# A frequency mixer and a two-layer network on one core: tokens stored n1 outside and n2 inside, and the order table rewritten

## The chip, the cores and the metric

The kernel runs on one core of a Trainium2 chip. A core has a TensorE for matrix products, a VectorE (DVE in the profile), a ScalarE (ACT) and a GpSimd (POOL) for elementwise work, a SyncE (SP) that issues transfers, and 16 DMA engines that carry them. SBUF holds the tiles on chip, in 128 partitions; PSUM takes TensorE's results, in eight banks of 512 fp32 columns per partition; HBM is the memory outside. The metric is the device time of one execution in microseconds (us). The three runs before the change took 845.41, 846.81 and 847.99 us, a median of 846.81.

## The reference

The input x is 8 sequences of 3008 tokens with 256 channels. A first part mixes in the frequency domain, a second is a network applied to each token. All in float32, with `w_in` of 256 x 2048 and `w_out` of 2048 x 256:

```python
X = np.fft.rfft(x, axis=1)
Yr = Xr @ w_r - Xi @ w_i + b_r
Yi = Xr @ w_i + Xi @ w_r + b_i
Yr = np.sign(Yr) * np.maximum(np.abs(Yr) - 0.01, 0.0)   # and Yi likewise
y = np.fft.irfft(Yr + 1j * Yi, n=3008, axis=1)
h = y.reshape(24064, 256) @ w_in
g = s * np.maximum(h, 0.0) ** 2 + b
out = g @ w_out                                         # 24064 x 256
```

## The kernel before

**The transform.** A sequence's 3008 tokens are laid out as n = 32 n1 + n2, with n1 from 0 to 93 and n2 from 0 to 31, and the transform over n is split into one over n1 and one over n2, each a matrix product with a constant table. For each batch (one sequence) there are four steps:

- `s1_units`: x (loaded by POOL's queue) times `A_t` over n1 gives u, which is evicted, written to the HBM buffer `ud` by SP and read back in another order as four loads `us`.
- `s23_units`: `fwd_unit` transforms `us` over n2 into xf, `sum_unit` and `mix_unit` apply the channel weights in three products, `shrink` does the soft threshold with three VectorE operations in the tile `ring`. Four small SBUF to SBUF transfers (`ring<-ring`, issued by SP; copies on VectorE for the last pairs of a batch) then exchange halves of the partitions, and `inv_unit` (matmuls `ring,T_t`) transforms back over n2 into v. v goes to HBM as `vd`, and two half loads `vs` bring it back in another order.
- `s4_units`: `vs` times `C_t` transforms back over n1. For up to five n2 at a time one PSUM bank takes 5 x 94 columns, and an eviction (`leave_bank`, a cast on ScalarE or VectorE) puts them into the tile `yt`, which holds y transposed: channels in the partitions, tokens along the row. For batches 2 to 7 a POOL copy puts the tokens with n1 from 80 to 93 into `tail`, shared by two batches.

Batch 0 goes through `first_batch`, which keeps it on chip; its first transposed result `ut` is evicted with a permuted access pattern already.

**The network.** The tokens are cut into 48 tiles of up to 512 (`_tile_order`): "wide" ones of batches 0 and 1 (16 n2 by 32 or 30 n1), "main" ones (32 n2 by 16 n1) and "tail" ones. `first_mm` makes h in PSUM (`psh<-yt,w_in`, 16 times two matmuls for each tile), each pair of banks is passed through a relu into `rt` and a square into `gt`, on ScalarE or VectorE, and the next tile's slots run the second product. In `second_mms` that is sixteen matmuls for each sub-tile of 128 tokens, into half a `psa` bank. In `seven_mms`, used for 21 tiles, seven products on sums of blocks stand in for eight; the sums are made by `s_op` on VectorE, and the fourth of them by an accumulating transfer on POOL's queue (`gt<-gt`, L1282). VectorE leaves the result in one of three tiles `ost` with two sub-tiles each, and `store` sends it to HBM by SP. A sub-tile's 128 tokens were eight n2 by sixteen n1 in a main tile, so a store's rows lay 32 rows apart in the output; two sub-tiles took two transfers. In tail tiles a sub-tile was cut at whole n2, into three pieces or so.

**The order.** The program of TensorE is one fixed list of 7662 matmuls, in which `plan` and `schedule` place the transform's units among the network's. Everything that the other engines and queues do from the second batch on is a "piece" made by `later`. Each engine, and each queue that issues transfers, works strictly in the order in which its pieces are issued, and waits at the head for what the piece needs. That order is written out by hand in `TURNS`, two characters in base 36 for every piece:

```python
at = [divmod(int(TURNS[k : k + 2], 36), 4) for k in range(0, len(TURNS), 2)]
... for k in sorted(range(len(at)), key=lambda k: k + at[k][0])
```

The quotient says by how many pieces the piece is put off, the remainder which engine does it (0 ScalarE, 1 VectorE, 2 SP, 3 POOL). `pump`, called ahead of every matmul, issues the pieces in that order as far as they have been made. Nothing else places the work: a load that the table issues late is late.

The functions that the diff touches, with what calls them:

Of the kernel before, what the change touches and what calls it, by code (L numbers as in the profile page):

```python
# [10 lines left out]
F16 = mybir.dt.float16  # L11
# [4 lines left out]
P = 128  # L16
N1 = 94
# [9 lines left out]
    "25253y20241x21251w26241s24242e1p2h3m363m2q1d20181c1k1x1o1h20213g1g1x251w30232j231s1g1s1t3o1s"  # L27
    "2x341t222a1k1k1t1k1t1w1x2w1w2d1x21252p4i5u2m2y143c1c1h1h1p1t1x2a66425m0o1h101c2x1c2c191i2q15"
    "191h1h1q5e2m320k111c1l111p1x215i4u222y0o1k2o0s3p0s191x25255662262m0g340h1d0d0g2q101t10181x3a"
    "2i2l0l1t25314e5y324y091m080w3c590h10390w1g4x0x191p1t2q1q3652044i0h0g1d0k1p0p151t1x5i522m5i0g"  # L30
    "3y0k0o1o11221a0k0s291c2s111h1t2h2i4m3m4u0h1a0k0w3c0z0x1p19252529462i52220g0o0w0p321820382h2y"
    "3a11191d1h2h2x193x082y0w143t151h212l31312d2d0x1m0s1431194a142g1g1s1u1s2c2d2q2u1d1k1w2i362u15"
    "1t1d3y181x1l2h251k2d1l1u2m20221k291x2l1k25241s2d213a1w20212a2e1x211k34212b1o301s2l2v1p1t2l1g"
    "1k2o1h2d1l2u1w291l1x2035251u2h5h1s2t1p1p1o1t1s2l1s1s3u1s2c2h2h1h2q3e1i1q102d45101k2w181d1h2d"
    "2n1c1l1c2o1m2x371l1p1x1p1g381w251l1s251x20291w3k1v2t2t1t1x1x313a3i4i3q101g191t0w1c1w1l2x131l"
    "1o201l2t1l2y3i1y2u2l2t11151c2g191h3x414e4q4a4y21270k200s1x2b0x0x1l113d0k1w191d0w28141g2w1d2h"
    "1b1l2x414h4y5e524e0w1s0x151c1i111w1d1c241d1l111m1u121y11211d1c311g1o2g1s1x1h1w2x1x2d35393q3a"
    "463m18421542102t111a1i0s10102p1525142h15144m1c1g2w1w2h1x1o1s2t323a1h1p1t294a2u3m2u0r1c1s0w2m"
    "0t2y1019281h1l1k211l2028353i3m1p1t1x293x2d3t353p2d3l2d0o0u0x120k25150w1g1h4i1o2s1c1x321s1w29"
    "2e2m1d1g1h2s1k2i321t22191l1k2s1x1w1w292u2a2e1l4e1g1t252d1o201t2021252e1s201t262e252t1l1o251t"  # L40
    "2x331s1s3o1s2p371l1p1x1c1g291o2l1o1q1s291t24242h21461x2p1s1w1w212d1p1s1w2k1w1z461s251p1p2l2a"
    "1q2i2u1l2p1o2k181l31371h1l1c2s5m1p292r1h1l35182h182g1l2p1g1p1g341l1p25292y2m3e221418241b1c2t"
    "1d3o1t211h1o251s2821253p3t56463y3m131d1c1x1d1l111u22121a182x1d142s1c1g341g1x1l2t3539524a4i36"
    "0s2o0x1215143g112q2a101x0x0w240z151h2s1c1l1p292d2l464e2m2u182h0x2m1d1c1s1h2q2610251p1c1x1k2c"
    "2g1s251p252h2h2p2u46323e1d42182s152218181c2d1l2a32111c1d5q1o3d1l1p25292h3l3d2t2t2x1p290k0o14"
    "1d4u0n1452142s1c1o1p2s1p2i1y181e1c1d521h241p2q3m1h1g1l1k1q1g1w1k1t2k1x2i1y1g2i2a1c1x1d2l411t"
    "211o3i1s2k1t1s211p1y2a1g1u2l2p1l3g1k1k2t2z1k1o351o2l331h1l2t181c2p1d2t1o1i1o2l1s1w1w30241u25"
    "2p1s1w2s1t1t1s281x2g1s234q1x241x251x3a3m261q3d3t1g1s1d1h1x271d1d1c2k1e2l2z1d1d2d1p1c341s2d25"
    "1o2d1p1x2d1s291v4t5121252l2t3u2y4e32101c1d1d0s181c1d2l4z1l141g111h1h3e2m1u2m2d3h0s1d0w281d2p"
    "3p3x4a5a4q4a151j0c2s0k1t230p0t1x142p0g10250x102c191c3c1o25131p292l2p3m323q2m182s0x191d3e101l"  # L50
    "1c1k2k1l1p1t3a2m2q261c3l1d1h2h1k1p311o2h1l1s2k1p1t2d353q4a4a3q0w4e104a1c1w1p1y220x0w0x240s2l"
    "141c151d2q1h1h1t1s2p2c1s2l252a2u1h2p353h3q4m3e420r1c1s101a112y1d1c2g191k1838151c4d2h322i151d"
    "1l1x2p4d2d411p392929082a151m041w1l0s1w1o461t2t1o1p3u1k1w292q2a1d1h1g281x2a3e192e181l1s2x241s"
    "241p2a1q2a2l2q1h1w1x2h1s2s1t1w21202q1w251t222e2h3l1o1s241t252b1t1w3k1w2h2r1p1t291g1k2t1o2h1s"
    "1u1s2c1p20252l204q21311o1s2t21251k1l1o1w1p5z3y1s1s1x211l262q1i3a1l1p182k1g1p213f181l1c2t261l"
    "1v1l1x211k1o2c212h291k281l252d20283v1t5p1x1x21293m322q2618291d1l10181k202h171t1s2829291l2u3m"
    "4a2q4u1y4a4u1a2e0m2u1t210p0x0k1o0p2x454d564m5a4a1h1r041w0k151z050d210s1p001s1l0t10251d1g1o20"
    "2d171t252d2h363q422e102c1t2114221429181s2c2d2d1h322m2e1a182t1t1k2s1t1s2x1w2h1l1s2p1p2d2p3d52"
    "4i4a3u114e104i101k1x262a0s0s142l0t0x101k15181e1d1g2t1p2p1k1s242d322m1h292d2l2y2q3u3a0r18390w"
    "2a182e1c1c2o1h1l1k1w1p28382l2q3e1l1p1t212x4d3h3t213h1l310k1m10220c1o151d1p1g4a1g2o1k1t3e1o1w"  # L60
    "1x2q2y1d1p1p1x1k1m3i1k3y1k1t1w2p1t1t1w1p2e1u2y1h2a1g2s1p1x1k1w20212g21321w251t2a1y2p2x1o1w3h"
    "1l1t271o1s3c1w2d2n1p1t2l1g1k381k291o1q242c1t1w1x351w4i1x1w2o1t1t1s201o2c1l1z4e1t1x212l1x2y32"
    "1u2y1429181h181p1g1s4e1w1x251s2d1w201t20251w243z2l451l361q2i1u363i111921293u4a3e3q0c0o0t0w1o"
    "181l0r1x1k1x1h2y1i353t1p1t183k1l212t3p524i3q3y0x1b0s141c1x270x11210w3l0w1s2111141s1d1x241w29"
    "1f1t292x313a565a3e1c1p1d1p1842181c1g1k211p29192u2e1y1i101p1p142w1k1l251k2l1l1w2k1t292h2t424i"
    "362q153u141e1g34252i2a1110141c112p1c2s1h1g4i1l1o2c1s2l1p1t242l2u361l1t393h423e4e3y0n101s0x12"
# [1455 lines left out]
```

## Time and profile before

| | |
|---|---|
| runs | 845.41, 846.81, 847.99 us |
| profiled execution | 845.85 us, its span 844.1 us |
| TensorE busy | 821.6 us, 97% |
| VectorE busy | 729.1 us, 86% |
| ScalarE busy | 705.8 us, 84% |
| POOL busy | 84.5 us, 10% |
| issues on SP's hardware queue | 100578 packets, 80.55 MB, 33.5% of the 16 DMA engines' span |
| stores of the output | 228 issues by SP |

The span is the time from the first to the last instruction of one execution; the execution's own time has 1.75 us around it. Each engine's busy time leaves out waits and the issuing of transfers. A group in the profile is named by engine, operation and tiles: `psh<-yt,w_in` is a matmul from yt and w_in into a PSUM tile psh. Behind a vertical bar stand the group's busy time in us and the mean of one in ns, and behind a second bar how long the engine had been idle ahead of them, and what ended that. In a list of waits the numbers are the total in us, how many times, and the longest. In the table of stretches each row has the stretch, its length, the busy time of TensorE, of its weight loads, of VectorE, ScalarE and POOL, each with its number of instructions, and then the granted TensorE clock as a share of full speed, the DMA engines' share and GB/s. For one tile the three durations in ns are the shortest, the median and the longest. The chain follows the work that ended last back from the end; its columns are start, duration and what it was.

### The profile page before, as it was taken

The numbers are of one execution on the slowest core, as the hardware profiler recorded it, in microseconds if no ns is written. First come the engines' busy times: TensorE is split into PE (matmuls) and PEld (weight loads), VectorE is DVE, ScalarE is ACT, GpSimd is POOL, SyncE is SP. The second block draws the span as 40 slices with busy tenths as digits, with TensorE's granted clock in tenths as the row PEclk, the third lists the DMA queues.
The fourth block names the chain that finished last, engine by engine and source line by source line (L and its number), as shares of the span: only waits on it lengthen the run. The fifth ranks groups of instructions, "written<-read, shape, count | busy, mean of one in ns | idle before, by whom it ended". The sixth has DMA issues, their size and how long they took to land.

```text
span 844.1 us, 19222 instructions
## 1 busy us (share of the span) xinstructions
PE 821.6 (97%) x7662; PEld 601.3 (71%) x7662; DVE 729.1 (86%) x1178; ACT 705.8 (84%) x888; POOL 84.5 (10%) x112
## 2 busy tenths in 40 slices
PE   8999999999999999999999999999999999999997
PEld 7857767777676767777677766767667777767765
DVE  5987889989898889999889889889879988889794
ACT  4988978998888888887899887988899988879773
POOL 4530000110012000110001100100002000011000
PEclk8999999999999999999999999999999999999999
DMA  8954537655458347574466543654556432623321
GB/s 198 177 153 97 125 109 191 133 132 124 116 142 179 100 119 216 115 148 115 114 162 159 126 123 108 168 143 110 133 161 158 92 88 66 162 56 65 77 66 54
DMA packets 114748, 107.14 MB, mean 127 GB/s; under 512 B 10854, under 2 KB 98922, under 8 KB 113314
## 3 DMA queue, kind: packets, MB, share of 16 engines
q1 hardware_dynamic: 100578, 80.55, 33.5%
q0 software_dynamic: 14080, 25.37, 18.4%
q8 instruction: 60, 0.98, 0.5%
q14 instruction: 30, 0.25, 0.1%
HBM read 53.52 MB, written 46.66 MB: 119 GB/s over the span
## 4 chain that ended last, share of the span: by engine, by line
PE 77%; DMA 11%; DVE 7%; ACT 3%; issue 1%; SPq 1%; POOL 0%; DVEq 0%; ACTq 0%; POOLq 0%
PE psh L235 31%; PE psa L235 28%; PE psf L235 16%; DMA ring<-ring 3%; DMA vs<-vd 3%; DMA gt<-gt 2%; DMA vd<-v 2%; PE psm L235 1%; DVE gt L1138 1%; ACT rt L1125 1%; ACT gt L1136 1%; DVE ring L891 1%; DMA x<-in_x_dram 1%; DVE rt L1127 1%; DMA us<-ud 1%
## 5 line engine op out<-in xcount | busy, mean ns | idle before, releaser
L235 PEld LDWEIGHTS <-gt 128*128 128x128 f16 (+1 forms) x3696 | 305.0, 101 | 170.1 <-DMA gt<-gt 2.9
L235 PE MATMUL psh<-yt,w_in 128*128 128x512 f16 (+1 forms) x1344 | 397.5, 378 | 1.2 <-DVE yt L298 0.8
L1125 ACT ACTIVATE rt<-psh 128x1024 f32<-128x1024 f32 (+2 forms) x322 | 323.8, 1007 | 72.7 <-PE psh L235 67.6
L235 PE MATMUL psa<-w_out_t,gt 128*128 128x256 f16 (+3 forms) x2448 | 310.0, 253 | 2.4 <-DMA gt<-gt 2.4
L1136 ACT ACTIVATE gt<-rt 128x1024 f16<-128x1024 f32 (+2 forms) x249 | 256.0, 1042 | 6.6 <-DVE rt L1127 4.5
L1138 DVE TENSOR_TENSOR gt<-rt 128x1024 f16<-128x1024 f32 (+2 forms) x135 | 161.2, 1202 | 5.7 <-ACT rt L1125 5.1
L235 PEld LDWEIGHTS <-w_in 128*128 128x128 f16 x1536 | 136.3, 98 | 28.0 <-issue 5.2
L1127 DVE TENSOR_SCALAR rt<-psh 128x1024 f32<-128x1024 f32 (+1 forms) x62 | 74.1, 1197 | 21.3 <-PE psh L235 14.9
L1282 POOL DMA_DIRECT2D gt<-gt x42 | 38.3, 938 | 514.3 <-DVE yt L298 93.1
L235 PE MATMUL psa<-T_s,gt 128*128 128x128 f16 (+1 forms) x944 | 79.4, 219 | 0.0
L891 DVE TENSOR_TENSOR ring<-psf,s 128x512 f16<-128x512 f32 x84 | 57.6, 686 | 21.4 <-PE psf L235 15.8
L235 PE MATMUL psh<-tail,w_in 128*128 128x512 f16 (+1 forms) x192 | 52.1, 353 | 0.0
L235 PEld LDWEIGHTS <-xf 128*128 128x128 f16 x504 | 46.9, 98 | 5.3 <-DVE xf L851 0.8
L235 PE MATMUL psf<-W_g,xf 128*128 128x256 f16 x336 | 50.4, 273 | 0.0
L298 DVE CAST u<-psf 96x512 f16<-96x512 f32 x53 | 36.0, 680 | 8.7 <-PE psf L235 8.5
L1225 DVE SCALAR_TENSOR_TENSOR ost<-psa,s_bc,bias_bc 128x512 f32<-128x512 f32 (+2 forms) x51 | 36.9, 723 | 6.5 <-PE psa L235 4.8
L298 ACT CAST xf<-psf 128x512 f16<-128x512 f32 x59 | 34.1, 583 | 8.9 <-PE psf L235 8.8
L235 PE MATMUL psf<-x,A_t 94*96 94x512 f16 x102 | 38.9, 382 | 0.9 <-DVE ring L891 0.5
L235 PE MATMUL psf<-C_t,vs 96*128 96x94 f16 (+1 forms) x484 | 37.7, 205 | 2.1 <-DMA vs<-vd 2.1
L298 ACT CAST yt<-psf 128x470 f16<-128x470 f32 (+2 forms) x70 | 35.7, 519 | 4.2 <-PE psf L235 2.9
L1325 DVE SCALAR_TENSOR_TENSOR ost<-psa,s_bc,zz 128x256 f32<-128x256 f32 (+1 forms) x80 | 36.2, 478 | 3.2 <-PE psa L235 2.0
L298 ACT CAST v<-psf 128x512 f16<-128x512 f32 x43 | 25.0, 583 | 14.2 <-PE psf L235 14.2
(121 smaller groups left out, 887.0 us busy)
## 6 DMA issues: line engine op xcount, KB each, us to landing
out_dram<-ost SPq DMA_DIRECT2D x152, 128.0 KB
ud<-u SPq DMA_DIRECT2D x56, 192.0 KB
us<-ud SPq DMA_DIRECT2D x28, 384.0 KB
vd<-v SPq DMA_DIRECT2D x42, 256.0 KB
vs<-vd SPq DMA_DIRECT2D x14, 768.0 KB
x<-in_x_dram POOLq DMA_DIRECT2D x28, 376.0 KB, 7.4
gt<-gt POOLq DMA_DIRECT2D x38, 256.0 KB, 4.7
ring<-ring SPq DMA_DIRECT2D x120, 64.0 KB
```

Source lines behind the costliest of these rows:

```text
L235: return nc.tensor.matmul(out, lhs, rhs, **how)
L298: (nc.scalar.copy if e == "act" else nc.vector.tensor_copy)(out=dst, in_=src)
L891: lambda e: nc.vector.tensor_tensor(out=ring[0][:, i % 4], in0=ps, in1=hold[i // 2][:, i % 2].unsqueeze(1).to_broadcast([P, 2, D]), op=ALU ...
L1125: nc.scalar.activation(out=rt, in_=ps[:, :, 0:w], func=AF.Relu)
L1127: nc.vector.tensor_scalar(out=rt, in0=ps[:, :, 0:w], scalar1=0.0, scalar2=None, op0=ALU.max)
L1136: nc.scalar.activation(out=gt, in_=rr, func=AF.Square)
L1138: nc.vector.tensor_tensor(out=gt, in0=rr, in1=rr, op=ALU.mult)
L1225: nc.vector.scalar_tensor_tensor(out=osts[number % 3][0:size, 0:k], in0=ps[0:size, 0:k], scalar=s_bc[0:size], in1=bias_bc[0:size].unsqueez ...
L1282: nc.gpsimd.dma_start(out=a12, in_=a11, accum_op=ALU.add)
L1325: nc.vector.scalar_tensor_tensor(out=out, in0=of, scalar=s_bc[0:size], in1=other, op0=ALU.mult, op1=ALU.add)
```

## The change

`yt` and `tail` hold the tokens with n1 outside and n2 inside. The evictions into `yt` read the PSUM bank in permuted order and write for each n1 the four or five n2 that the bank holds. A main tile's 16 n1 by 32 n2 tokens are then 512 neighbouring elements of the row, in the order of the output's rows. `store` is called once for two sub-tiles, and sends 256 consecutive rows by one transfer where it can; wide tiles keep one for each sub-tile, or two where a sub-tile ends inside an n1. All of `TURNS` is replaced: 2440 entries in place of 2525; the 85 that are gone are stores. The matmuls and their order stay.

```diff
@@ first_batch, last_dft
-        yt = yts[0] = ypool.tile([P, DC, N2, 96], F16, name="yt", tag="yt")
+        yt = yts[0] = ypool.tile([P, DC, 96, N2], F16, name="yt", tag="yt")
...
-                yt[:, ec, n : n + 4, :], ps,
-                ps[:, 0:384].rearrange("p (j n) -> p j n", n=96), 384,
+                yt[:, ec, :, n : n + 4], ps,
+                ps[:, 0:384].rearrange("p (j n) -> p n j", n=96), 384,
@@ s4_units
-                yt[:, ec, n2 : n2 + w, 0:N1], ps,
-                ps[:, 0 : w * N1].rearrange("p (j n) -> p j n", n=N1), w * N1,
+                yt[:, ec, 0:N1, n2 : n2 + w], ps,
+                ps[:, 0 : w * N1].rearrange("p (j n) -> p n j", n=N1), w * N1,
...
-                        out=tails[pr][:, :, half], in_=yt[:, :, :, 80:94]
+                        out=tails[pr][:, :, half], in_=yt[:, :, 80:94, :]
@@ rhs_of
-            return yts[b][:, dc, HW * h : HW * h + HW, lo : lo + w]
+            return yts[b][:, dc, lo : lo + w, HW * h : HW * h + HW]
         if kind == "main":
-            return yts[b][:, dc, :, 16 * j : 16 * j + 16]
-        return tails[b][:, dc].rearrange("p h n m -> p (h n m)")[:, j : j + w]
+            return yts[b][:, dc, 16 * j : 16 * j + 16, :]
+        return tails[b][:, dc].rearrange("p h m n -> p (h m n)")[:, j : j + w]
@@ store
-    def store(tl, sub, number, i, op):
-        src = osts[number % 3][:, i, :]
+    def store(tl, sub, k, number, op):
+        src = osts[number % 3]
...
         if kind == "wide":
             h, lo = j
-            n2 = HW * h + 4 * sub
-            rows = out[b * N : (b + 1) * N, :].rearrange("(n1 n2) d -> n2 n1 d", n2=N2)
-            send(rows[n2 : n2 + 4, lo : lo + w], src[0 : 4 * w])
+            rows = out[b * N : (b + 1) * N, :].rearrange("(n1 n2) d -> n1 n2 d", n2=N2)
+            rows = rows[:, HW * h : HW * h + HW]
+            for i in range(k):
+                t = (sub + i) * size
+                end = t + size
+                while t < end:
+                    n1, n2 = divmod(t, HW)
+                    whole = n2 == 0 and end - t >= HW
+                    cnt = (end - t) // HW * HW if whole else min(HW - n2, end - t)
...
         if kind == "main":
-            rows = out[b * N + 512 * j : b * N + 512 * (j + 1), :]
-            send(rows.rearrange("(n1 n2) d -> n2 n1 d", n2=N2)[8 * sub : 8 * sub + 8], src)
-            return
+            runs = [(b * N + 512 * j + P * sub, P * k)]
+        else:
...
+        if len(runs) == 1 and runs[0][1] == P * k:
+            rows = out[runs[0][0] : runs[0][0] + P * k]
+            send(rows.rearrange("(i p) d -> p i d", p=P), src[:, 0:k])
+            return
...
@@ second_mms
-                for i in range(k):
-                    store(tl, sub - k + 1 + i, number, i, op)
+                store(tl, sub - k + 1, k, number, op)
@@ seven_mms, leave
-                    for j in range(2):
-                        store(tl, 2 * i + j, hold["o", 3 * i], j, op)
+                    store(tl, 2 * i, 2, hold["o", 3 * i], op)
@@ the table, its first entries
-    "25253y20241x21251w26241s24242e1p2h3m363m2q1d20181c1k1x1o1h20213g1g1x251w30232j231s1g1s1t3o1s"
+    "28292i242d21282g2l2q1w1x2h252i1o2h3e3m423m1k281k1o1o281t1h251k301h1s29202d371j3b251o21243h1s"
```

## The prediction, written before the result was known

> **What bounds the kernel now.** I read the first part of the page, then the busy time by stretches, then TensorE's waits, the chain in order of time, and the groups that the change rewrites.
>
> ```profile
> PE 821.6 (97%) x7662; PEld 601.3 (71%) x7662; DVE 729.1 (86%) x1178; ACT 705.8 (84%) x888; POOL 84.5 (10%) x112
> ```
>
> ```profile
> 58.00:200.00 142.00, 139.73 (x1268) 103.32 (x1267) 126.05 (x222) 123.41 (x160) 10.79 (x15) 1.00 0.57 134
> 200.00:400.00 200.00, 194.61 (x1789) 141.72 (x1788) 178.50 (x287) 167.78 (x209) 15.79 (x20) 1.00 0.57 141
> 400.00:600.00 200.00, 197.03 (x1811) 142.42 (x1809) 177.24 (x284) 174.06 (x217) 15.49 (x20) 1.00 0.55 134
> 600.00:800.00 200.00, 199.12 (x1906) 144.17 (x1905) 173.10 (x269) 172.97 (x205) 14.42 (x16) 1.00 0.42 106
> ```
>
> TensorE is the bound: busy 139.7 of 142, 194.6 of 200, 197.0 of 200, 199.1 of 200 us, at a granted clock of 1.00. No matmul is added or dropped, so a gain can only come from TensorE's pauses. From the matmuls' starts (each form has one usual distance to the next; the excess is a pause) the pauses sum to 26.0 us, 15 of them after us 58. TensorE's waits name the enders:
>
> ```profile
> PE psf L235 <- DMA ring<-ring: 2.7, 4, 1.2
> PE psa L235 <- DMA gt<-gt: 2.4, 3, 0.9
> PE psf L235 <- DMA vs<-vd: 2.1, 3, 1.3
> PE psf L235 <- DVE xf L298: 1.5, 1, 1.5
> ...
> PE psf L235 <- DMA us<-ud: 0.7, 1, 0.7
> ```
>
> Four kinds of transfer that land late. Counted by matmul starts, pauses behind a late transfer are 9.7 us after us 58: ring copies 3.4, gt sums 2.85, vs loads 2.55, us loads 0.9. The chain shows how long such landings last:
>
> ```profile
> 223.81 5.01 DMA vd<-v
> ...
> 228.90 5.86 DMA vs<-vd
> ...
> 265.34 7.29 DMA ring<-ring
> ...
> 332.31 7.65 DMA gt<-gt
> ```
>
> Each queue works in the order that the table gives: if the table puts a transfer 7 us ahead of its matmul and it needs 8.5, TensorE pauses 1.5.
>
> **The change part by part.** The sum is made against the profiled execution's own 845.85 us (span 844.1, 1.75 around it), 0.96 below the median of 846.81.
>
> *Layout of yt.* The matmuls read 512 neighbouring elements in place of 32 runs of 16.
>
> ```profile
> L235 PE MATMUL psh<-yt,w_in 128*128 128x512 f16 x1216 | 361.0, 379 | 1.2 <-DVE yt L298 0.8 <-DVE rt L1127 0.2
> L235 PE MATMUL psh<-tail,w_in 128*128 128x512 f16 x96 | 28.6, 379 | 0.0
> L249 DVE CAST ut<-psf 128x384 f16<-128x384 f32 x8 | 4.5, 558 | 8.1 <-PE psf L235 8.0
> L298 DVE CAST yt<-psf 128x384 f16<-128x384 f32 x4 | 2.2, 545 | 0.0
> ```
>
> The tail is read in one run today and costs 379 ns as well: worth 0. The evictions into yt now read PSUM by jumps and write runs of 5 (of 4 in the first batch). The ut eviction does that with runs of 4: 558 ns against 545 on VectorE; on ScalarE 479 against 485 to 489. So about +13 ns for each of some 39 on VectorE, 0.5 us in all, and -6 to -10 ns on ScalarE: hidden, as between an eviction's end and the matmul that needs it the trace leaves a median 0.8 us (under 0.4 us in 9 of 102). If every one took 0.25 us more, those gaps would let through 0.2 us. I take 0; ends -0.1 and +0.5, the upper for runs of 5, which no row shows. [...] POOL's six tail copies (median 1.17 us) are issued 26 us or more before use: 0.
>
> *Stores.* From the code: 228 issues become 143. Main tiles: 59 of 256 rows and 2 of 128 for 120 of 128; tails 18 for 60; wide tiles 64 for 48, since a sub-tile of 120 tokens no longer ends on a whole n1 and is sent as 112 + 8.
>
> ```profile
> L1162 SPq DMA_DIRECT2D out_dram<-ost x228: 248/609/1142, 65.3 to 840.0; - x114
> L966 SPq DMA_DIRECT2D vd<-v x42: 355/424/936, 89.6 to 717.7; - x42
> ```
>
> SP issues stores for 135 of its 307 us. The nearest row for a 256 KB store is vd's write (256 KB from 128 partitions, 0.42 us); a store keeps 0.61 at the worst. 65 x 0.42 + 48 x 0.61 + 30 x 0.35 = 67 us, or 80 with 0.61 throughout: 55 to 68 us less on SP, which was not the bound (307 of 844). On the path lies only what queues behind stores. By the trace's landing records a main store took a median 3.1 us and its semaphore climbed in 9 steps, a wide one 5.2 us in 5 steps, vd's write 3.3 us in 16 steps for twice the bytes; I read the steps as 8, 4 and 16 DMA engines at work. Two stores of 3.1, the second issued 0.6 later, become one of about 3.3. Half a us less in front of a ring copy takes a quarter to a third off the late sum of the ring copies; I take -0.7 us (ends 0 and -2.5).
>
> *The table.* Two characters per piece of work in base 36; the number over 4 is by how many pieces it is put off, the remainder its engine. Old and new first entries, "25" and "28", are 77 and 80: 19 pieces late on VectorE, 20 late on ScalarE. I decoded both, matched the pieces (2525 less 85 stores is 2440), and took as slack the time from the matmul in front of which a transfer is issued to the matmul that needs it, in the profile's matmul starts:
> - vs loads: shortest slack 6.8 us, now 9.4; under 9 us: 5 of 14, now 0. With the needs measured (queueing plus landing, 6.5 to 12.0) the late sum falls from 8.9 to 2.0 if needs and slacks are combined at random, so three quarters of 2.55: -2.0 us. One at us 234.8 (1.47 us) keeps its 10.3 us, as its v write lands late.
> - us loads: the late one at us 553.5 has 14.1 us in place of 6.5: -0.8.
> - gt sums: the late ones at us 340 and 374 gain 1.5 and 1.6 us of slack, that at 790.5 none: -2.1 where they stand, -1.3 by the same random pairing (2.04 to 1.13). I take -1.3.
> - ring copies: the shortest goes from 3.4 to 5.2, but more groups are near the edge: the last copy of a group has under 7 us in 24 of 40, before in 17. At random the late sum falls 16%, -0.5; with each copy's own lateness kept it grows from 2.5 to 8.0, +5.5. The copies' new neighbours on SP are fewer, which speaks for the first; I take 0, ends -3.4 and +5.5.
> - engines: 12 relus and 8 evictions go to VectorE, 5 squares back: 12 x 1.22 + 8 x 0.68 - 5 x 1.23 - 0.7 = +13 us on VectorE (86 to 88% busy), some -13 on ScalarE. Six pieces (squares, ring moves on VectorE, sums of the seven products) now have less slack than they took, together 3 us; each lay in another order, so I take +1.0 (ends 0 and +3). What is late next is psa's leaving: shortest slack 3.3, now 2.2 us, against 0.7 to 2.9 taken.
> - the end: the last out's store still stands ahead of two ready ones; the third starts 0.2 to 0.4 sooner: -0.3 (ends +0.3 and -1).
>
> A 3.15 us VectorE square at us 450.3 (usual 1.23) beside POOL's tail copy cost the wait on xf, 1.5 us; it may go or recur: 0, ends -1.5 and +1.5.
>
> Sum: 0 - 0.7 - 2.0 - 0.8 - 1.3 + 0 + 1.0 - 0.3 = -4.1; 841.75 in the profile's own terms, with 0.96 back 842.7 at the median: 842.5.
>
> **The rivals.**
> - *The ring copies turn late* (slower). Place: TensorE's ring,T_t matmuls of batches 1 to 7. For it: 24 of 40 groups under 7 us while half of them need 5 or more; VectorE, which runs the shrink ahead of them, is fuller by 13 us. Against: fewer stores, less time in front of them. Price: +5.5 with each copy's lateness, +10.4 with half a us more; with the other terms' -4.1 + 0.7 that is +2.1 to +7, so 849 to 854. It decides where the copies land, against their plan, as late as today.
> - *The pauses only change places.* The late transfers go and others come, within 2.5 us: 844.5 to 849. For it: both tables fill VectorE over its time in some stretches of 20 us, and the pauses before were placed by chance too. Against: the slacks of vs and us grew at every short place.
> - *Spread stores carry more.* If the stores on few engines are what stretches ring copies to 7.29 us (median 2.6), all four kinds shorten: -9.7 of late transfers, -1 at the end, 836 to 838. [...]
> - *Slow evictions.* If the runs of 5 cost 0.4 us more, 84 of them put 34 us on two engines that are idle 14 to 16%; the gaps let through 0.8 us directly, a tenth of the load 3 more: 847.
>
> **How the numbers follow.** What a measurement of this kernel tells from no change is 0.3%, 2.5 us: 844.3 and 849.4 are the bounds. Forecast (839 to 844.2): 0.58. Spread stores: 0.06. Changed places: 0.15, taken as the same. Ring copies late: 0.17, slower, 0.02 of it inside the bound. Slow evictions or some other stretch: 0.04, slower in most. So faster 0.63, same 0.17, slower 0.20. The range from 838 to 851 leaves out the better half of the spread case and the worse half of the ring case, less than 2 in 10; the forecast's own is 839 to 844.
>
> **What would show it.** In the profile after: the waits of TensorE on vs and us gone but for one near us 235, gt at most one; psh<-yt still 379 ns; yt evictions 545 to 560 ns (ScalarE) and 640 to 660 (VectorE); out_dram<-ost x143, near 0.42 us for the large ones; ring copies' waits at 2 to 4 us. Wrong it would be with ring waits above 6 us, waits of psa matmuls on VectorE's ost, or evictions over 0.75 us.

## The result and the profile after

The changed kernel took 836.2 us (835.52, 836.88, 838.0, 834.68) against 846.11 us for the kernel before (845.41, 846.81, 847.99, 844.2): a ratio of 0.9884 with a 95% interval from 0.9852 to 0.9916. Two later comparisons of the same two kernels gave 0.9864 (0.9833 to 0.9895) and 0.9871 (0.9842 to 0.99). So it is faster by 1.2 to 1.4%, some 10 to 11 us, where 4 us were forecast, and its time lies below the predicted range. One slow execution, 1218.26 us of the kernel e10 below, is left out of all figures. The profiled execution is the one of 835.52 us, with a span of 833.7. The profile's first part, then TensorE's busy time by stretches (the columns as before: stretch, length, busy time and instructions of TensorE, its weight loads, VectorE, ScalarE and POOL, then clock, DMA share and GB/s):

```profile
PE 818.9 (98%) x7662; PEld 598.5 (72%) x7662; DVE 736.8 (88%) x1192; ACT 702.2 (84%) x874; POOL 83.4 (10%) x112
```

```profile
58.00:200.00 142.00, 141.44 (x1286) 105.38 (x1285) 127.39 (x226) 126.71 (x164) 10.04 (x14) 1.00 0.55 129
200.00:400.00 200.00, 197.98 (x1805) 143.30 (x1803) 182.34 (x292) 171.36 (x209) 16.00 (x20) 1.00 0.56 138
400.00:600.00 200.00, 199.36 (x1830) 144.41 (x1829) 181.41 (x290) 172.15 (x215) 14.88 (x20) 1.00 0.55 140
600.00:800.00 200.00, 199.37 (x1921) 143.99 (x1919) 179.86 (x277) 168.59 (x194) 14.77 (x17) 1.00 0.39 102
```

TensorE pauses for 0.56, 2.02, 0.64 and 0.63 us in the four stretches; before it was 2.27, 5.39, 2.97 and 0.88. VectorE is a little fuller, 88% in place of 86. TensorE's waits (total in us, times, longest):

```profile
PE psf L234 <- DMA ring<-ring: 1.3, 2, 0.8
...
PE psf L234 <- ACT yt L297: 0.6, 2, 0.3
PE psa L234 <- DMA gt<-gt: 0.6, 2, 0.4
```

The rows for vs, us and xf, 2.1, 0.7 and 1.5 us before, are gone from the list, and gt went from 2.4 to 0.6, ring from 2.7 to 1.3.

**Three parts of the span.** All the kernels below run the same 7662 matmuls in the same order, so a span can be cut by them: *start* up to matmul 600 (there the first batch's evictions into yt differ, in runs of four that take as long as before, and with the new order also the order of each engine's last dozen or so operations), *middle* from there to the start of the last matmul, *end* from there on.

| profile of | start | middle | end | span |
|---|---|---|---|---|
| before | 62.1 | 775.7 | 6.2 | 844.1 |
| after | 60.5 | 768.5 | 4.8 | 833.7 |
| after, second profile | 61.2 | 767.3 | 4.8 | 833.2 |
| after, third profile | 64.6 | 767.5 | 4.8 | 836.9 |

The start varies by itself, 60.3 to 64.6 us over all profiles here, so the 1.6 us at the start, of 10.3 between the first two profiles, tell nothing of the change. The middle gave 7.2 to 8.4 us, the end 1.5. The pauses in the middle, counted by matmul starts as in the prediction, can be sorted in two ways. By what ended them, those behind late transfers were 3.4 us for ring copies, 2.85 for gt sums, 2.55 for vs and 0.9 for us loads; in the three profiles after they are 1.0 to 1.9, 0.5 to 1.2, 0 and 0. By the matmul that paused, whatever ended its wait, they went so: matmuls on vs from 2.6 to 0.9, second products (psa) from 2.9 to between 1.6 and 2.2, matmuls on ring from 4.6 to between 2.5 and 3.0, matmuls on us from 1.5 to 0.6, and one wait of 1.7 us on a VectorE result at us 454 is gone. What is left at the matmuls on vs is no vs load: those waits end with ScalarE evictions into yt. Pauses at vs, gt, ring or us below are sorted in this second way.

**What was left alone, and what grew.** Groups with their count, busy time, mean in ns and the idle time ahead of them, of the changed kernel:

```profile
L234 PE MATMUL psh<-yt,w_in 128*128 128x512 f16 x1216 | 360.8, 379 | 1.5 <-ACT u L297 0.8 <-DVE rt L1124 0.3 <-ACT rt L1122 0.2
L297 ACT CAST yt<-psf 128x470 f16<-128x470 f32 x52 | 34.0, 683 | 2.9 <-PE psf L234 2.7
L297 DVE CAST yt<-psf 128x470 f16<-128x470 f32 x32 | 22.4, 704 | 3.4 <-PE psf L234 3.4
L297 DVE CAST yt<-psf 128x384 f16<-128x384 f32 x5 | 2.7, 546 | 0.0
L297 ACT CAST yt<-psf 128x384 f16<-128x384 f32 x4 | 2.0, 488 | 1.5 <-PE psf L234 1.5
```

and of the kernel before:

```profile
L298 ACT CAST yt<-psf 128x470 f16<-128x470 f32 x56 | 30.5, 556 | 4.0 <-PE psf L235 2.9
L298 DVE CAST yt<-psf 128x470 f16<-128x470 f32 x28 | 18.0, 642 | 4.4 <-PE psf L235 4.3
```

The matmuls on yt still take 379 ns. The evictions of 470 columns, which write runs of five, take 127 ns more on ScalarE and 62 more on VectorE in the mean; those of 384 columns, in runs of four, are unchanged (546 to 545, 488 to 485). The mean hides two kinds, as the shortest, median and longest of the changed kernel's evictions show:

```profile
L297 ACT CAST yt<-psf x60: 302/604/838, 34.8 to 729.7; 128x470 f16<-128x470 f32 x52, 128x384 f16<-128x384 f32 x4, 128x188 f16<-128x188 f32 x4
L297 DVE CAST yt<-psf x47: 342/643/821, 32.8 to 730.9; 128x470 f16<-128x470 f32 x32, 128x188 f16<-128x188 f32 x10, 128x384 f16<-128x384 f32 x5
```

Sorted by the first n2 of the run, the 84 evictions of 470 columns have these means in ns (a row of 32 tokens takes 64 bytes):

| first n2 | bytes in the row | ScalarE (before 551 to 563) | VectorE (before 639 to 646) |
|---|---|---|---|
| 0 | 0 to 9 | 580 | 648 |
| 5 | 10 to 19 | 828 | 818 |
| 10 | 20 to 29 | 598 | 644 |
| 15 | 30 to 39 | 767 | 745 |
| 20 | 40 to 49 | 756 | 732 |
| 25 | 50 to 59 | 579 | 642 |

Nearly all the cost lies with three of the six places, those whose ten bytes run across a multiple of 16 in the row; the other runs of five cost next to nothing, and the eight bytes of a run of four, which begin at multiples of eight, never run across one. No kernel here cuts the runs elsewhere to test this. On the path the slower evictions show a little: the matmuls on vs pause 0.9 us behind ScalarE's evictions into yt in each profile after, and not at all in e2 below, which has the new order with the old evictions. (Of the 0.6 us listed above on an eviction into yt, 0.3 stood before too.)

### The profile page after: what moved, and what is told of

It is laid out like the page before. It is cut to its first block, busy times and chain, and to the rows that moved or that the text cites. A ratio compares the mean times of both kernels' runs of the same rounds, so it can differ in the third digit from the quotient of the medians.

```text
span 833.7 us, 19076 instructions
## 1 busy us (share of the span) xinstructions
PE 818.9 (98%) x7662; PEld 598.5 (72%) x7662; DVE 736.8 (88%) x1192; ACT 702.2 (84%) x874; POOL 83.4 (10%) x112
## 4 chain that ended last, share of the span: by engine, by line
PE 83%; DVE 8%; DMA 5%; ACT 2%; issue 1%; POOL 0%; SPq 0%; DVEq 0%; ACTq 0%; POOLq 0%
PE psh L234 34%; PE psa L234 31%; PE psf L234 17%; DMA ring<-ring 2%; DMA gt<-gt 2%; DVE rt L1124 1%; DMA x<-in_x_dram 1%; PE psm L234 1%; DVE gt L1135 1%; ACT rt L1122 1%; DVE u L297 1%; DVE yt L297 1%; DVE gt L1276 1%; DVE ring L934 0%; POOL x L370 0%
## 5 line engine op out<-in xcount | busy, mean ns | idle before, releaser
L1122 ACT ACTIVATE rt<-psh 128x1024 f32<-128x1024 f32 (+2 forms) x310 | 311.4, 1006 | 63.1 <-PE psh L234 55.7
L1133 ACT ACTIVATE gt<-rt 128x1024 f16<-128x1024 f32 (+2 forms) x254 | 261.6, 1041 | 11.4 <-DVE rt L1124 8.6
L1135 DVE TENSOR_TENSOR gt<-rt 128x1024 f16<-128x1024 f32 (+2 forms) x130 | 154.3, 1194 | 7.7 <-ACT rt L1122 7.0
L1124 DVE TENSOR_SCALAR rt<-psh 128x1024 f32<-128x1024 f32 (+2 forms) x74 | 88.2, 1193 | 19.9 <-PE psh L234 17.5
L297 ACT CAST xf<-psf 128x512 f16<-128x512 f32 x52 | 30.3, 585 | 10.1 <-PE psf L234 9.9
L297 ACT CAST u<-psf 96x512 f16<-96x512 f32 x54 | 31.0, 578 | 6.7 <-PE psf L234 5.4
L297 ACT CAST v<-psf 128x512 f16<-128x512 f32 x49 | 28.6, 583 | 9.3 <-PE psf L234 9.1
```

The costliest lines, as they stand in the source:

```text
L297: (nc.scalar.copy if e == "act" else nc.vector.tensor_copy)(out=dst, in_=src)
L1122: nc.scalar.activation(out=rt, in_=ps[:, :, 0:w], func=AF.Relu)
L1124: nc.vector.tensor_scalar(out=rt, in0=ps[:, :, 0:w], scalar1=0.0, scalar2=None, op0=ALU.max)
L1133: nc.scalar.activation(out=gt, in_=rr, func=AF.Square)
L1135: nc.vector.tensor_tensor(out=gt, in0=rr, in1=rr, op=ALU.mult)
```

## The experiments

Each row is a kernel; the ratio is to the kernel before, run on the same chip in the same comparison. In the last three columns are the parts of its one profile. e1 to e4, e5 to e8, e9 to e12 and e13 to e16 ran together, on four chips.

| kernel | what it is | median us | ratio (95%) | start | middle | end |
|---|---|---|---|---|---|---|
| e1_old_order | new stores and layout, old order | 841.05 | 0.9931 (0.9903 to 0.9959) | 63.2 | 772.5 | 4.0 |
| e2_old_stores | old stores and layout, new order | 850.49 | 1.0066 (1.0043 to 1.0088) | 60.8 | 780.3 | 7.0 |
| e3_two_stores_8 | after, 256 rows as 2 x 128, 16 engines | 836.92 | 0.9896 (0.9858 to 0.9933) | 63.8 | 769.4 | 4.9 |
| e4_end | after, last stores by readiness | 836.34 | 0.9881 (0.9842 to 0.9919) | 63.9 | 768.3 | 3.5 |
| e5_strided_8 | after, strided stores, 8 engines | 841.48 | 0.9950 (0.9929 to 0.9970) | 61.1 | 771.4 | 9.0 |
| e6_strided_16 | after, strided stores, 16 engines | 837.51 | 0.9895 (0.9861 to 0.9929) | 60.3 | 768.5 | 5.8 |
| e7_after_again | the changed kernel | 834.88 | 0.9864 (0.9833 to 0.9895) | 61.2 | 767.3 | 4.8 |
| e8_order_loads | before, loads and gt sums earlier | 843.13 | 0.9967 (0.9944 to 0.9991) | 60.8 | 771.5 | 6.3 |
| e9_tail_later | before, one POOL copy later | 844.47 | 0.9973 (0.9951 to 0.9994) | 60.8 | 774.5 | 6.1 |
| e10_old_moved | e1 with the moves of e8 and e9 | 835.82 | 0.9890 (0.9861 to 0.9920) | 60.8 | 769.1 | 4.0 |
| e11_end_again | e4 | 834.0 | 0.9853 (0.9825 to 0.9881) | 61.7 | 767.2 | 3.5 |
| e12_after_third | the changed kernel | 835.23 | 0.9871 (0.9842 to 0.9900) | 64.6 | 767.5 | 4.8 |
| e13_new_order_8 | e5, lone stores strided too | 839.98 | 0.9918 (0.9894 to 0.9942) | 61.2 | 771.3 | 7.1 |
| e14_new_order_16 | e6, lone stores strided too | 839.44 | 0.9920 (0.9891 to 0.9949) | 60.8 | 768.6 | 6.4 |
| e15_old_order_8 | e1, strided stores, 8 engines | 847.64 | 1.0019 (0.9999 to 1.0039) | 61.9 | 777.9 | 6.5 |
| e16_old_order_16 | e1, strided stores, 16 engines | 841.77 | 0.9944 (0.9923 to 0.9966) | 60.7 | 776.4 | 5.7 |

### The stores or the order

The change has two separable parts, the stores (with the layout that they need) and the order. e1 takes the new stores with the old order: only the table differs from the changed kernel, a merged store standing where the first of its pair stood. The put-offs in a table are relative to the pieces, so every entry changes; the first ones:

```diff
 e1 against the changed kernel, TURNS only
-    "28292i242d21282g2l2q1w1x2h252i1o2h3e3m423m1k281k1o1o281t1h25
+    "01012m0008010109000e08000g0c1601111y1q1u1a010g0000000h08010g
...
```

> The changed kernel with the old order of the work: the old table's sequence and engines, each pair's single store at the place where the pair's first store stood. Theory 'order' (the gain is the table's longer lead of vs, us and gt transfers): the waits behind late transfers stay, 9.7 us of them less about 1 that shorter stores take from ring copies, so 844 to 847, near the kernel before. Theory 'stores' (stores on 8 or 4 DMA engines stretched the other landings): the late transfers go with the old order too, 837 to 840. A price of the 5-wide evictions (ScalarE 683 ns in place of 556, VectorE 704 in place of 642) would show as more than 846, as the old order was written for the shorter ones.

e2 is the reverse, the old layout and stores with the new order. Where a pair or a cut tail store had been merged, its two or more stores all stand at the place of the merged one:

```diff
 e2 against the kernel before, TURNS only
-    "25253y20241x21251w26241s24242e1p2h3m363m2q1d20181c1k1x1o1h20
+    "00010i000901000k0x0y00010l0d0y000x1y1y2i26000s0000000s09010l
...
```

> The kernel before with the new order: old layout of yt, old evictions, two stores of eight times sixteen rows per pair at the place of the new single store. Theory 'order': 836 to 839, TensorE's waits on vs and us gone, gt at most 1 us. Theory 'stores': late ring copies, vs and gt loads stay for more than half of their 9.7 us, 842 to 846.

e1: 841.05 us, 0.69% (5.8 us; by the interval 3.5 to 8.2) better than before with the order untouched; the two medians of this comparison, 845.05 and 841.05, lie 4.0 apart. So about half of the whole gain comes without the new order, and it was forecast at 1.0 us (0.7 and 0.3 at the end). The middle is 3.2 us shorter, the end 2.2.

e2: 850.49 us, 0.66% slower than before. One place makes most of it. Its longest wait, and the stretches around us 565:

```profile
PE psf L235 <- DMA ring<-ring: 7.8, 3, 5.9
```

```profile
560.00:565.00 5.00, 4.54 (x51) 3.33 (x48) 4.22 (x8) 5.00 (x7) 2.16 (x4) 1.00 0.86 157
565.00:570.00 5.00, 0.00 (x0) 0.00 (x0) 0.00 (x0) 0.52 (x1) 0.72 (x2) 0.86 1.02 207
570.00:575.00 5.00, 4.56 (x26) 3.06 (x27) 4.38 (x6) 1.92 (x3) 0.00 (x0) 0.50 0.29 62
```

SP issues eight cut tail stores from us 558.1 to 563.6, among and ahead of two ring copies of us 561.5 and 563.6, which land 7.4 and 6.7 us after their issue (median 2.6 before). TensorE stands for 5.9 us, and afterwards its granted clock is 0.50, so in the next 5 us it runs 26 matmuls (of mixed shapes) where the first row has 51. The bunch is where I had put the split stores, so e2 is no fair price of the order alone. It does show how a few small stores can hold up what is issued behind them: in e13 below, with the same order and main stores on 8 engines but two merged stores at this place, the same two ring copies are issued 2.8 and 3.6 us earlier, counted from the ring copy ahead, land after 3.8 and 3.1 us, and TensorE doesn't stop there.

### What about the stores: engines, issues or rows

By the landing records a main store of the kernel before takes a median 3.1 us for 128 KB with 9 steps of its semaphore, the new one of 256 KB takes 2.6 us with 16. The packets near the end, where only stores run, bear out the reading of these steps as 8 and 16 engines: of the store that the kernel before issues at us 835.42 most often 8 are under way at a time, of that at us 829.80 in the changed kernel 16. Below, "8 engines" and "16 engines" are read from the steps in the same way. Three things differ: how many DMA engines carry a store, how many issues there are, and whether the rows are consecutive. e3 was meant to leave the rows and go back to 8 engines:

```diff
-            send(rows.rearrange("(i p) d -> p i d", p=P), src[:, 0:k])
+            rows = rows.rearrange("(i a c) d -> i a c d", a=8, c=16)
+            for i in range(k):
+                send(rows[i], src[:, i])
```

> The changed kernel, only that every store of 256 consecutive rows is two of 128, each in eight groups of sixteen rows, as the stores before were cut, so that 8 DMA engines and two issues carry them; layout, order and evictions are the changed kernel's. Theory 'order': within 1.5 us of the changed kernel, 836 to 838; store landings near 3.1 us again and 65 more issues on SP cost little. Theory 'stores': 839 to 843, with ring copies' landings above 6 us at one in ten again.

It missed its aim: the 8 and the 16 are consecutive in memory, and the landing records show 16 steps, as many as those of the changed kernel's eight single stores of 128 consecutive rows. What it does test is one issue or two on 16 engines: 836.92 us at 0.9896, within its interval of the changed kernel's 0.9864 to 0.9884. One issue less for each pair is worth nothing that can be measured.

e5 and e6 store a main pair by two strided transfers whose rows can't be merged, over 8 and over 16:

```diff
+            if kind == "main" and k == 2:
+                block = out[b * N + 512 * j : b * N + 512 * (j + 1), :]
+                block = block.rearrange("(n1 n2) d -> n2 n1 d", n2=N2)
+                for i in range(k):
+                    q = sub + i
 e5:
+                    send(block[8 * q : 8 * q + 8], src[:, i])
 e6:
+                    send(block[16 * (q % 2) : 16 * (q % 2) + 16, 8 * (q // 2) : 8 * (q // 2) + 8], src[:, i])
+                return
```

> The changed kernel, only that each 256-row store of a main tile is two of 128 rows sent to the rows that the kernel before would have used (eight groups of sixteen rows, 32 rows apart), so that rows of the output come out permuted; tails, layout, order and evictions as changed. It has 59 more issues and stores on 8 DMA engines. Theory 'stores' (spread over 16 engines is what the new order lives on): 839 to 843, late ring copies and gt sums growing from 5 to 8 us or more between matmul 600 and the last. Theory 'order and merging do not need it': 836 to 838, as the two stores on 16 engines gave. The long last-but-one run with all old stores had nine cut tail stores ahead of two ring copies; if those alone made it slow, this one stays near 837.

> As the kernel before it in this call, but each of the two stores covers sixteen groups of eight rows, 32 rows apart, so that 16 engines carry it to scattered rows (rows of the output permuted). If the number of engines matters it is as quick as the changed kernel, 835.5 to 837.5, and the one with 8 engines slower; if scattered rows matter, both are slow alike, 839 or more; if neither, both are near 837.

> The changed kernel unchanged, to stand beside the others on one chip: 835 to 837. If its start (matmul 600 at 60.5 us in its first profile, 62 to 64 in the others) is chance, it can be at 62 to 64 here with the same stretch after it, 768 to 769 us from matmul 600 to the last.

841.48, 837.51 and 834.88 us on one chip, in the order expected if engines count. But e5's end takes 9.0 us, and there the comparison is spoiled: its last lone stores, still of consecutive rows, write rows that the strided ones had written (and leave other rows of that tile unwritten), and SP issued one store at 835.06, just after an earlier one had landed at 835.04, and another at 838.53, after 838.51. In e6 those rows don't overlap. e6, with scattered rows on 16 engines, is still 2.6 us above e7, and their executions hardly overlap (836.49 to 839.17 and 834.52 to 836.68): 1.0 of it is in the end, 1.2 in the middle. As two issues of whole rows cost nothing measurable in e3, the scattered rows are the likelier cause; no run tests them alone. e13 to e16 repeat the pair with the lone stores strided as well (the condition without `k == 2`), once in the new order and once in the old:

> The new kernel with all main tiles stored by strided transfers of 8 n2 by 16 n1 rows (8 engines each), the lone ones of the last tile too, so that no store at the end has to wait for an earlier one that writes the same rows, as two did in the earlier strided run on 8 engines. The output's rows stand in another order. Theory A, the number of engines is what counts: the stretch between matmul 600 and the last stays near 771 us, the end comes to near 6 us, median 838.5 to 840, 1.5 to 3 us above the 16-engine twin. Theory B, the earlier loss was the wait at the end: within 1 us of the twin, 837 to 838.5.

> The twin on 16 engines: strided transfers of 16 n2 by 8 n1 rows for all main tiles, as many issues and rows of the same size. The output's rows stand in another order. Both theories: near the earlier 16-engine run, 836.5 to 838, the stretch between matmul 600 and the last near 768.5 us.

> The old order of issue with the new layout; main tiles stored by two strided transfers on 8 engines at the places that the old order gives them, tail and wide tiles as in the new kernel. The output's rows stand in another order. Theory A: nearly the kernel before, 0.997 to 1.001 of it, 843.5 to 846. Theory C, that the whole rows and fewer issues of tail tiles bring the gain: 0.993 to 0.996, 840 to 843.

> The same on 16 engines, 16 n2 by 8 n1 rows in each transfer. The output's rows stand in another order. Theory A: the gain of the new stores in the old order comes back, 0.992 to 0.995, 839 to 842, 2 to 4 us below the 8-engine twin. Theory C or the single issue of 256 rows as the cause: no better than the twin by more than 1 us.

In the old order the answer is plain. With 8 engines the new layout has no gain at all (1.0019), with 16 it has 0.56%, and 5.9 us lie between the medians, as much as e1 gained over before. (The two kernels also send different blocks of rows, 8 n2 by 16 n1 and 16 n2 by 8 n1; that this matters was not ruled out.) e1, with whole rows and half the issues, stands at 0.9931 beside e16's 0.9944: in this order nothing measurable is left for these two. In the new order the step is not shown by the times: the medians differ by 0.5 us only, with overlapping intervals. The middle is 2.6 us shorter in the profiles (e14 to e13; 2.9 from e6 to e5), but e13's profile is its slowest execution, e14's among its fastest. e5's larger distance was largely its end.

What the 16 engines change is seen in the landing of other transfers. SP's own land a little sooner in e16 than in e15 (medians from issue to landing: vd 2.8 us for 3.2, us 4.6 for 5.1, vs 6.6 for 7.0; ring copies of 64 KB 2.4 for 2.5), and so do those of another queue. The issues of gt sums on POOL's queue (count, KB each, median us from issue to landing), of the kernel before and e15 (the same row), of e16, and of the changed kernel:

```profile
gt<-gt POOLq DMA_DIRECT2D x38, 256.0 KB, 4.7
```

```profile
gt<-gt POOLq DMA_DIRECT2D x38, 256.0 KB, 4.3
```

```profile
gt<-gt POOLq DMA_DIRECT2D x38, 256.0 KB, 4.0
```

No store is ahead of these in their queue, and yet the gt sums land 0.4 us sooner when main stores go over 16 engines. All 18 profiles agree: 4.6 to 5.2 us in the seven kernels with main stores on 8 engines, 4.0 to 4.5 in the eleven profiles with 16. The x loads on the same queue don't separate so (7.0 to 7.6 and 6.2 to 7.4). TensorE's waits for gt sums and ring copies, in e15 and then in e16:

```profile
PE psa L235 <- DMA gt<-gt: 4.3, 4, 1.9
PE psf L235 <- DMA ring<-ring: 2.9, 4, 1.3
```

```profile
PE psf L235 <- DMA ring<-ring: 3.5, 3, 1.3
PE psa L235 <- DMA gt<-gt: 2.1, 3, 0.9
```

The gt waits halve, those for ring copies don't. But the kernel before, on 8 engines too, had gt waits of 2.4 us, and e9 below 3.7, so one profile of each proves little here. The largest single difference between the two profiles, 2.0 us, is a gt sum needed at us 342, which pauses TensorE in e15 and not in e16. e16's profiled execution, 844.54 us, is the slowest of its seven, so the two profiles differ by less than the medians; which waits carry the 5.9 us is not shown. In the new order it is the matmuls on ring that differ: their pauses are 6.3 and 7.0 us with 8 engines (e5, e13) and 3.6 and 4.3 with 16 (e6, e14).

### The loads and gt sums of the new table

e8 leaves the kernel before as it is and moves, in its table alone, vs loads, us loads and gt sums ahead, each to the matmul at which the new table issues it or as near as what it needs allows: nine vs loads, seven us loads and twenty gt sums came earlier. The shortest slack of the vs loads rises from 6.8 to 9.8 us, that of the us loads from 6.5 to 7.6, the mean of the gt sums from 8.7 to 9.3.

```diff
 e8 against the kernel before, issue order as TURNS gives it
+ vs (9), us (7), gt sum (20): at the new table's place
  ...
- vs (9), us (7), gt sum (20): at the old table's place
```

> The kernel before with old layout and old stores; of its order only the late loads move: 9 vs loads, 7 us loads and 20 gt sums are issued earlier, to the lead that the new order gives them (shortest lead of vs 6.8 to 9.8 us, us 6.5 to 7.6). My step on the table (vs -2.0, us -0.8, gt -1.3): 840.5 to 842.5 if those pauses are worth what stands in the profile and nothing else becomes late. If the pauses only change places (a queue's head waits for a transfer that is issued too early): 844 to 847.

843.13 us, 0.33% (2.8 us; 0.8 to 4.7), less than the 4.1 that the prediction gave these three, and the prediction's sum within the interval. TensorE's pauses at vs went from 2.6 to 1.6 us, at gt from 2.9 to 1.3, at us from 1.5 to 0.7; the profile is that of the fastest of the twelve executions (840.45 us).

### The VectorE operation beside POOL's copy

The kernel before had a square on VectorE of 3.15 us in place of 1.23 at us 450.3, which I had left at 0 as something that may go or recur. Rows of its timeline (start, duration, engine, what):

```profile
450.28 3.15 DVE L1138 TENSOR_TENSOR gt<-rt 128x1024 f16<-128x1024 f32 x1
...
450.76 1.58 POOL L1037 COPY tail<-yt 128x896 f16<-128x896 f16 x1
...
454.08 0.38 PE L235 MATMUL psf<-F_t,us 128*128 128x128 f16 x4 [1.51 <-DVE xf L298]
```

The square ends at 453.43, 1.09 us after the copy's end at 452.34: it looks as if it had done its work only then. The gap before the same matmul was 1.68 us in before, e1, e15 and e16 and 1.41 in e8, where another operation (`zz<-zz,b`, 2.08 us for 0.42) met the copy; it is absent from all kernels with the new order. So it belongs to the order and does not come by chance. e9 tests it by itself; the issue order on POOL's queue, as the table gives it:

```diff
 e9 against the kernel before, POOL's order in batch 4
- copy tail<-yt
  load x
  load x
+ copy tail<-yt
```

> The kernel before, with one piece moved: batch 4's copy into tail on POOL (at us 450.76 in its profile) goes behind the next two x loads on POOL's queue, some 1.2 to 2.5 us later. Theory 'copy beside an SBUF operation': the VectorE square that took 3.15 us at us 450.3 takes 1.23 again and the pause of 1.68 us in front of matmul 4115 is gone; the stretch from matmul 600 to the last is 774 us in place of 775.7. Rival 'chance, or the DMA issues on POOL beside it': the square stays near 3 us, since gt and x issues still stand beside it.

844.47 us, 0.27% (0.06 to 0.49) better; in the profile the middle is 1.2 us shorter, the pause of 1.68 gone and those at gt 1.4 longer. In its timeline:

```profile
447.92 1.22 DVE L1138 TENSOR_TENSOR gt<-rt 128x1024 f16<-128x1024 f32 x1
...
449.47 1.61 POOL L1037 COPY tail<-yt 128x896 f16<-128x896 f16 x1
...
450.05 0.39 PE L235 MATMUL psf<-F_t,us 128*128 128x128 f16 x4
...
450.65 0.59 DVE L851 TENSOR_TENSOR xf<-xf 128x256 f16<-128x256 f16 x1
```

The square is back at 1.22 us and the matmuls wait for nothing. The copy now meets an `xf<-xf` sum, which takes 0.59 in place of 0.28 us and holds nobody up. The three VectorE operations that read PSUM beside the same copy took their usual times, 0.68, 0.68 and 0.47. The four stretched operations named here all have both inputs in SBUF: the square (3.15 us for 1.23), `zz<-zz,b` in e8 (2.08 for 0.42), this sum (0.59 for 0.28) and one in the changed kernel below (1.68 for 0.28). Not every operation of this kind was stretched: in the kernel before a square at us 543.3 took its usual 0.95 us beside a copy. What holds them up was not shown. By the recorded starts the VectorE operation began 0.26 to 0.48 us ahead of the copy in before, e8 and the changed kernel, and still it was the one that was held up.

The new order has such a meeting too. Rows of the changed kernel's timeline:

```profile
342.78 1.68 DVE L850 TENSOR_TENSOR xf<-xf 128x256 f16<-128x256 f16 x1
...
343.04 1.26 POOL L1036 COPY tail<-yt 128x896 f16<-128x896 f16 x1
...
346.32 0.47 DVE L1333 SCALAR_TENSOR_TENSOR zz<-psa,s_bc,zz 128x256 f32<-128x256 f32 x1
...
346.84 0.33 PE L234 MATMUL psa<-T_s,gt 128*128 128x128 f16 x3 [0.30 <-DVE zz L1333]
```

The sum takes 1.4 us more than its usual 0.28. VectorE then works without a gap up to the `zz` at 346.32, for which TensorE waits 0.30 us (0.46 by matmul starts). The wait stands in all three profiles of the changed kernel; that moving the copy would remove it was not tried.

### Together

e10 puts the pieces together on the old order: e1's stores, e8's moves, e9's move.

```diff
 e10 against e1, TURNS only
+ the moves of e8 and of e9
```

> New layout and stores with the old order, but with the loads moved earlier as in the run with old stores (9 vs, 7 us, 20 gt) and batch 4's tail copy behind two x loads: the terms found so far, put together. If they are the whole of the gain it comes within 0.25% of the changed kernel (834 to 838); if the rest of the new order carries something of its own, 838 to 842.

835.82 us, 0.9890, beside the changed kernel's 835.23 and 0.9871 in the same comparison. One by one they gave 0.69, 0.33 and 0.27%, 1.29 in sum; together 1.10%. The sum is not fully kept, as quicker landings and earlier issues mend some of the same waits: e1 alone already takes gt pauses from 2.9 to 0.7 us. The remaining 0.2% between e10 and the changed kernel is within the intervals, and I don't assign it.

### The end

In the changed kernel the last three stores are issued in an order in which the first waits for the last result, with a ready pair behind it:

```diff
 e4, e11 against the changed kernel, the last entries of SP
- store sub 3 of the last tile     (result ready last)
  store sub 0 and 1                (ready first)
  store sub 2
+ store sub 3
```

> The changed kernel with the last three stores in the order in which their data is ready, and not the last one first. Each of the two earlier stores then leaves before the last matmul is done, and the span's end follows one store in place of three: last landing 1.2 us sooner (now 832.78 at issues from 829.8, 830.2, 830.7), so 834.9 to 835.4 at the median, if nothing else ends the span.

> The changed kernel with the last three stores in the order of their data, beside the changed kernel itself on one chip: 1.3 us less than it (its profile had 3.49 us after the last matmul's start in place of 4.77), so 833.5 to 835.5 where the changed kernel is at 835 to 837.

> The changed kernel unchanged, for comparison on the same chip: 835 to 837; matmul 600 between 60 and 64 us, 767 to 769 us from there to the last matmul, 4.8 us after it.

In every profile the end is shorter by 1.3 us: 3.5 and 3.5 in e4 and e11, 4.8 three times in the changed kernel. The medians can hardly tell it: e4 836.34 (its profile has a start of 63.9), e11 834.0 beside 835.23 for the changed kernel in the same comparison. It is the fastest kernel here, by about what the profile shows and no more than the intervals allow.

## Why the prediction was wrong, step by step

- **Stores, -0.7 (ends 0 and -2.5), and the end, -0.3 (ends +0.3 and -1): the failed step.** Measured, both together in the old order: -5.8 us, 3.5 to 8.2 (-4.0 by the medians); the end alone was -1.5 in the changed kernel. The step priced "half a us less in front of a ring copy", that is SP's time. It left out what a store on few engines does to the landing of other transfers, such as the gt sums (median 4.7 us in e15, 4.3 in e16), though the landing records with 9 and 5 steps for a store, read as 8 and 4 engines, stood in the same paragraph: with main stores back on 8 engines (e15) nothing of the gain is left. The rival "Spread stores carry more" had this mechanism and got 0.06. That its figure, 836 to 838, was met is in part luck: it gave all 9.7 us of late transfers to the stores, and the stores alone came to 841.05. Its first clause ("if the stores on few engines are what stretches ring copies to 7.29 us") holds in part: ring copies fell from a ninth decile of 6.1 us to 5.3 in landing time, and in the new order the pauses that differ with the engines are at ring, while in the old order they stayed (4.6 before, 4.1 in e1).
- **vs -2.0, us -0.8, gt -1.3.** The pauses ended by these transfers fell by 2.55, 0.9 and 1.7 to 2.3 us, with the stores' part in it; by the order alone (e8) it was 2.8 us instead of 4.1. The mechanism was right, the size somewhat high.
- **Ring copies, 0 (ends -3.4 and +5.5).** Pauses at ring 4.6 before, 2.5 to 3.0 after: -1.6 to -2.1, in the range. With main stores on 8 engines in the new order they are 6.3 and 7.0. So the tight ring copies of the new order were a real risk, and in these profiles the stores on 16 engines took it away: the two parts of the change can't be priced apart.
- **The square beside POOL's copy, 0 (ends -1.5 and +1.5).** -1.7 in its gap, 2.3 by e9's ratio. The trace of before had VectorE and POOL side by side at that place. The new order has no such neighbours there, but has them at us 342.8, for 0.3 to 0.5 us.
- **Engines and new tight pieces, +1.0.** Added up, VectorE's operations take 12.7 us more, close to the 13 of the forecast (its busy time, which counts overlaps once, grew by 7.7); ScalarE's take 3.3 less, not 13, as its evictions into yt grew. Pauses ahead of the first product (`psh`) grew by 0.5 us (0.25 to 0.72), and small new ones came ahead of the second, 0.5 us behind `ost` (0.1 before) and 0.5 behind `zz`: some 1.4 in all, near the +1.0.
- **Layout, 0 (ends -0.1 and +0.5).** 0.9 us by the pauses at vs, past the upper end. The matmuls at 379 ns are as forecast; the evictions were forecast at 545 to 560 ns on ScalarE and 640 to 660 on VectorE and took 683 and 704 in the mean, so taking the 384-column row for runs of five was wrong for half of them.
- **Ring copies late, changed places, slow evictions.** Not as a whole: gt and ring waits fell, the new waits named here come to some 2.3 us, and 127 ns more for a ScalarE eviction let 0.9 us through.
- **The whole.** Singly the stores with the end gave -5.8 us, the loads and gt sums -2.8, the square -2.3, against -1.0, -4.1 and 0: the miss is the stores' 4.8 us and the square, less 1.3 at the loads. (The chances of the cases add up to 0.64 faster and 0.19 slower, where the prediction's last figures are 0.63 and 0.20.)

## What to carry to other kernels

Before pricing a change of a store by its issue time, count the DMA engines that it runs on (read here from 9 and 16 steps) and look at landing times in the other queues: here the same bytes on 16 engines in place of 8 were worth 5.9 us with one order of issue; with another the medians show 0.5 us, which is within their scatter. A single odd duration in a trace (3.15 us for 1.23) is worth asking what ran beside it: with both placed by a fixed order it came back in the kernels that kept the order there, and moving one of them took it away. A mean over a group can hide two kinds: look at the shortest and the longest too. And where two parts of a change work on the same waits, run each alone and both together, as they neither add nor stay apart.

## What the hardware showed that I had not expected

- Runs of five f16 cost an eviction of 470 columns 0.2 to 0.28 us on ScalarE and 0.09 to 0.18 on VectorE where the run's ten bytes cross a multiple of 16 in the row, and under 0.05 us elsewhere; runs of four (384 columns, 485 to 488 and 545 to 546) cost nothing, with the same jumps in PSUM.
- After a pause of 5.9 us TensorE's clock was granted at 0.50 for some 5 us (e2). Two idle times of 1.3 and 0.9 us close together, waits for ring copies at us 270 to 272, were followed by 3.4 us at 0.50 in e15 and in e16; in the kernel before the waits at this place were 0.2 and 1.2 us, and the clock stayed at 1.00 in all its stretches from us 58 to 800.
- The first 600 matmuls took between 60.3 and 64.6 us over the profiles, 60.5, 61.2 and 64.6 in three of the changed kernel itself; that spread is more than most of the edits are worth; only the cut by matmuls showed effects of 1 to 2 us. The four longest starts (63.2 to 64.6, in e1, e3, e4 and e12) have 3.4 us at a clock of 0.50 from some us 14.7 to 17.0 on; whether the clock lengthened them was not tested.
- What stays open: ring copies of the changed kernel still land late around us 260 (6.47 us in its chain) beside x loads issued a few us earlier; moving these was not tried.
